# A Strassen GLU with a spectral branch on one core: an addition, a weight step, bank reads and SBUF additions change places in hand-ordered queues, and one tile gets a second buffer

## The chip, the cores and the metric

The kernel runs on one core of a Trainium2 chip. The metric is the device time of one execution in microseconds; the time before is 1399.58 us, the median of three runs (1398.88 to 1401.85). A core has five engines that each work through a queue in order: TensorE (PE; its weight loads are listed as PEld), VectorE (DVE), ScalarE (ACT), GpSimd (POOL) and SyncE (SP), which here only issues DMAs. Engines wait for one another through semaphores, so an instruction that waits holds up everything behind it in its queue.

## The reference

```python
xn = layernorm(A_x)                        # (1, 2048, 576), no affine part
a  = irfft2(rfft2(xn) * (w_r + 1j * w_i))  # over both axes
h  = sigmoid(xn @ w_gate) * (xn @ w_up)    # 576 -> 4608
out = A_x + a + h @ w_down                 # 4608 -> 576
```

All is float32. The kernel splits each fp32 operand into a high part (fp32r) and a low part, the difference to the high part, and multiplies high by high, low by high and high by low.

## The kernel before, in words

**Units.** The first stage makes h. F = 4608 is cut into 36 blocks f of 128, and the 2048 rows into two halves p, each as two column blocks of 512. A unit (f, p) makes both the gate and the up product for its block with seven products instead of eight (Strassen's scheme in Winograd's form): P1 to P7, each a group of seven matmuls of 128x512 (`prod`, L360). They gather in three PSUM banks: A (P1, then P2 on it), B (a copy of A after P1, then P6, P7 and P4 on it) and E (P5, then P3 on it). Banks A and E have two buffers, B one. `unit` (L393) writes the order out by hand: P5, P6, P2, P7, then P1 of the next unit (`ahead`), then P4 and P3. Between them ACT copies or squashes bank B and A into h and g (L401, L405, L408, L411, L418), and DVE adds bank E to h: L415 adds P5's part to h[:, 1], and P3, which adds onto bank E, must wait until it has been read; L421 adds E with P3 to h[:, 0]; L422 multiplies by g.

**Besides.** Seven times in a unit `beside()` (L838) is called, and whatever it emits takes its place in the engines' queues there. It advances `make_w(f + 1)` (L221), which splits the next block's weights: three ACT copies (L213), their low halves on DVE (L217, L219), then the sums in place (L229, L231, L232), four ACT copies more and the low halves of w1 and w2. Five steps of it come in unit (f, 0), the rest in (f, 1), two steps a beside in its first two. There are 31 units of p = 1 that lead to a new block. It also calls `tick()`, which takes one step of each side job: `export` (L425), which sends h, its sums and differences (L439, L442, L445, L448) to DRAM for two blocks at a time, and `make_t` (L452), which splits w_down's blocks (L465, L467, and L476 to L482) and sends them to DRAM. In the last two units it advances `early()` (L802) too: the first loads of the second stage, its first high and low parts (`cut_hi`, L793 and L796; `cut_lo`, L798 and L800). From the third unit on PE, DVE and ACT run in exactly the written order; for units (2, 0) and (3, 0) a scheduler orders the instructions. The last four units are (34, 0), (35, 0), (34, 1), (35, 1).

**The second stage** multiplies h by w_down in the same seven products, now one after another: for product j, half p and block pair k (18 of them) one step n (L1215). A step fetches a piece of h for step n + 10, makes the high part for step n + 4 (ACT) and the low part for step n + 3 (DVE), and does 12 matmuls of 128x288 in four PSUM banks m0 to m3, one buffer each (`down`, L1198). At k = 0 and 16 banks m0 and m1 are done for two steps at once, at k = 1 and 17 banks m2 and m3. So m0 and m1 end one step before m2 and m3, and a step later m0 and m1 are written again. A finished bank goes to `evac` (L1133): an addition or copy out of the bank first, and, one step later (`emptied`, L1210), additions from SBUF to SBUF (two per bank for P7 and P5, one for P2 and P6). They are all L1142.

Beside it, `aside()` advances the spectral branch: `phase1b` (L918), 16 tiles, with normalisation into xb (L285), the even and odd parts eo (L929, one buffer, read by PE's transposes pf), the high and low parts (L906, L909), products pd and pa; `phase2` (L982) with L1015, L1017 and L1019; `phase3` (L1035), whose L1098 to L1101 add the result to acc and so free the bank that py or pe takes next. `landed` (L897) sends a finished row block out.

Of the kernel before, what the change touches and what calls it, by code (L numbers as in the profile page):

```python
# [9 lines left out]
F32 = mybir.dt.float32  # L10
# [3 lines left out]
OP = mybir.AluOpType  # L14
PSUM = bass.MemoryType.PSUM

P = 128
# [107 lines left out]
def spectral_glu_kernel(ctx: ExitStack, tc: tile.TileContext, x, w_r, w_i, w_gate, w_up, w_down, out):  # L125
# [231 lines left out]
    STEPS = ((0, 0), (3, 0), (0, 3), (1, 1), (4, 1), (1, 4), (2, 2))  # L357
    H = {}

    def prod(b, w, xx, start, stop, skip=False):  # L360
        for j, (sx, sw) in enumerate(STEPS):
            nc.tensor.matmul(b, w[:, sw, :], xx[:, sx, :], start=start and j == 0, stop=stop and j == len(STEPS) - 1,  # L362
                             skip_group_check=skip)

# [16 lines left out]

    B = {}

    def made(u, b, k, start, stop=True):
        f, p = u
        ka, kb = FACTORS[k]
        prod(B[u, b], weight(f, kb), get_x(p, ka), start, stop, not start)

    def ahead(u):
        B[u, "A"] = bank("bA", f"pA{u[0]}_{u[1]}", 2)  # L390
# [2 lines left out]
    def unit(u, beside, after):  # L393

        f, p = u
        h = new_h(f, p)
        g = run.tile([P, 2, CW], F32, tag="g", name=f"g{f}_{p}")
        B[u, "B"] = bank("bB", f"pB{f}_{p}")
        B[u, "E"] = bank("bE", f"pE{f}_{p}", 2)
        bA, bB, bE = (B[u, k] for k in "ABE")  # L400
        nc.scalar.activation(bB, bA, AF.Copy)  # L401
        made(u, "E", "P5", True)
        beside()
        made(u, "B", "P6", False)
        nc.scalar.activation(h[:, 0], bB, AF.Copy)  # L405
        beside()
        made(u, "A", "P2", False)
        nc.scalar.activation(g[:, 0], bA, AF.Sigmoid)  # L408
        beside()
        made(u, "B", "P7", False)  # L410
        nc.scalar.activation(h[:, 1], bB, AF.Copy)  # L411
        beside()
        if after:
            ahead(after)
        nc.vector.tensor_tensor(h[:, 1], h[:, 1], bE, op=OP.add)  # L415
        beside()
        made(u, "B", "P4", False)
        nc.scalar.activation(g[:, 1], bB, AF.Sigmoid)  # L418
        beside()
        made(u, "E", "P3", False)  # L420
        nc.vector.tensor_tensor(h[:, 0], h[:, 0], bE, op=OP.add)  # L421
        nc.vector.tensor_tensor(h, h, g, op=OP.mult)  # L422
        beside()

    def export(k, p):  # L425

        a, b = H[2 * k, p], H[2 * k + 1, p]
        A11, A21, A12, A22 = a[:, 0], a[:, 1], b[:, 0], b[:, 1]

        def put(what, src):  # L430
            nc.sync.dma_start(ssp[ORDER.index(what)][p][k], src)

        put("P1", A11)
        put("P2", A12)
        put("P4", A22)
        s = run.tile([P, 2, CW], F32, tag="s", name=f"s{k}_{p}")
        S1, S2 = (s[:, i] for i in range(2))
        yield
        nc.vector.tensor_tensor(S1, A21, A22, op=OP.add)  # L439
        put("P5", S1)  # L440
        yield
        nc.vector.tensor_tensor(S2, S1, A11, op=OP.subtract)  # L442
        put("P6", S2)
        yield
        nc.vector.tensor_tensor(A21, A11, A21, op=OP.subtract)  # L445
        put("P7", A21)
        yield
        nc.vector.tensor_tensor(A12, A12, S2, op=OP.subtract)  # L448
        put("P3", A12)
        yield  # L450

    def make_t(k):  # L452
# [349 lines left out]
    def early():  # L802
        for n in range(20):
            if n < 2:
                for i in range(3):
                    fetch(3 * n + i)
            else:
                fetch_t(0, n - 2)
            if 12 <= n <= 12 + CA:
                cut_hi(n - 12)  # L810
            if 13 <= n < 13 + CA:
                cut_lo(n - 13)
            yield
        for n in range(FS, FA):
            fetch(n)
# [5 lines left out]
    for i, u in enumerate(UNITS):  # L821
        if i == 2:
            written.enter_context(tc.manual_schedule(engines={nc.tensor.engine, nc.vector.engine, nc.scalar.engine}))
        f, p = u
        after = UNITS[i + 1] if i + 1 < len(UNITS) else None
        last = f >= NF - 2
        if i == 0:
            sides += [export(0, 1), factors(1)]
            make = make_w(3)
        elif (f, p) == (3, 1) or (f > 3 and p == 0 and f + 1 < NF):  # L830
            make = make_w(f + 1)
        if (f, p) == (NF - 2, 1):
            first.close()
            ring = late.enter_context(tc.tile_pool(name="ring", bufs=1, side="right", reuse_waits="tile"))
            soon = early()
        count = 0

        def beside():  # L838
            nonlocal count
            count += 1  # L840
            turn = after and after[0] != f
            for _ in range(2 if turn and (last or f == 3 or count < 3) else 1 if turn or f < 4 or count > 2 else 0):
                next(make, None)
            for _ in range(2 if turn and (last or count < 4) else 1):
                next(soon, None)
            tick()
            if turn and count == 7:
                finish(make)
            if i == 1 and count == 4:
                finish(*sides)  # L850

        unit(u, beside, after)
        if f % 2 == 1:
            sides.append(export(f // 2, p))
        if u == (3, 0):
            load_raw(4)
            load_raw(5)
        elif p == 0 and f >= 4 and f + 2 < NF:
            load_raw(f + 2)
        if u == (2, 1):  # L860
            sides.append(g for k in range(NPR) for g in make_t(k))
# [56 lines left out]
    def phase1b(t):  # L918
# [5 lines left out]
        for _ in range(6):  # L924
            yield
        norm(xb[:, :D], acc[t], t)
        eo = wide(pool, "eo", t)
        for e, op in ((0, OP.add), (1, OP.subtract)):
            nc.vector.tensor_tensor(eo[:, e, :HD + 1], xb[:, :HD + 1], xb[:, HD:D + 1][:, ::-1], op=op)  # L929
        yield  # L930
# [202 lines left out]
    def evac(what, p, m, b):  # L1133

        v = b[:, :HD]
        t1, t2 = tid(p, 0, m), tid(p, 1, m)

        def part(q):
            return acc[(t1, t2)[q // 2]][:, q % 2 * HD:(q % 2 + 1) * HD]

        def add(o, a):
            nc.vector.tensor_tensor(o, o, a, op=OP.add)  # L1142

        if what == "P1":
            U[p, m] = u = accp.tile([P, HD], F32, name=f"u{p}{m}")
            nc.scalar.activation(u, v, AF.Copy)
        elif what == "P2":
            add(part(0), v)
            yield
            add(part(0), U[p, m])  # L1150
        elif what == "P6":
            add(U[p, m], v)
            yield
            add(part(1), U[p, m])
        elif what == "P7":
            add(U[p, m], v)
            yield
            add(part(2), U[p, m])
            add(part(3), U[p, m])
        elif what == "P4":  # L1160
            add(part(2), v)
        elif what == "P5":
            w = accp.tile([P, HD], F32, tag="v", name=f"v{p}{m}", bufs=4)
            nc.scalar.activation(w, v, AF.Copy)
            yield
            add(part(3), w)
            landed(t2)
            add(part(1), w)
        else:
            add(part(1), v)  # L1170
            landed(t1)
        yield

    active = []

    def aside():
# [21 lines left out]
    def down(n, m):  # L1198
        j, p, k = seq[n]
        if k == 0:  # L1200
            M[m] = ps.tile([P, CW], F32, tag=f"m{m}", name=f"m{j}_{p}{m}")
        s, t, o = SP_[n], TT[j, k], M[m][:, :HD]
        for i, (a, b) in enumerate(((0, 0), (0, 1), (1, 0))):
            nc.tensor.matmul(o, s[:, a, m * P:(m + 1) * P], t[:, b, :], start=k == 0 and i == 0, stop=k == NPR - 1 and i == 2)  # L1204
        if k == NPR - 1:
            done.append(evac(ORDER[j], p, m, M[m]))

    done, out_of = [], []

    def emptied():  # L1210
        out_of[:] = [g for g in out_of if next(g, out_of) is not out_of]
        out_of.extend(g for g in done if next(g, done) is not done)
        done.clear()

    for n, (j, p, k) in enumerate(seq):  # L1215
        fetch(n + FA)
        for load in loads.pop(n, []):
            load()
        if n:
            cut_hi(n + CA)  # L1220
            cut_lo(n + CA - 1)
        emptied()
        if k in (0, NPR - 2):
            for m in range(2):
                down(n, m)
                down(n + 1, m)
        elif k in (1, NPR - 1):
            for m in range(2, TPC):
                down(n - 1, m)
                down(n, m)  # L1230
        else:
            for m in range(TPC):
                down(n, m)
        active.extend(b() for b in begin.pop(n, []))
        aside()
    while active or done or out_of:
        emptied()
        aside()
    assert not begin and not loads, (begin, loads)
    written.close()  # L1240
    two.close()
# [21 lines left out]
```

## Time and profile before

| | |
|---|---|
| median of the runs | 1399.58 us |
| the profiled execution | 1399.83 us |
| its span, first to last instruction | 1398.0 us |
| matmuls | 7827 |
| HBM over the span | 211 GB/s |

The span is cut as follows: up to about 105 us the start, hand-ordered but for its end; to about 856 us the units; after that the second stage with the spectral branch. In the lines of the timeline the first number is the start in us from the span's start, the second the length in us, then engine, line, operation and tiles, `xN` the number of instructions merged, and in brackets how long the engine stood before it and for whom. In the lines of waits: total in us, number, longest. In the lines by stage: stretch, length, then busy us and number of instructions of PE, PEld, DVE, ACT and POOL, granted clock of PE, share of the DMA engines, GB/s. The group lines of the page give busy us and mean ns, then the idle time ahead of them and who ended it. DVE's instructions overlap a little: the distance from start to start is shorter than the length shown.

### The profile page before, as it was taken

What the parts mean: (1) busy time and instruction counts of PE and PEld (TensorE: products, weight loads), DVE (VectorE), ACT (ScalarE), POOL (GpSimd) and SP (SyncE); (2) the same over time, 40 slices, a digit from 0 to 9 for tenths busy, and PEclk for the clock granted to TensorE, in tenths of its full rate; (3) what the DMA queues carried; (4) which work ended last, traced back from release to release, by engine and by line L of the source; (5) the groups of instructions that cost most, each with busy time, mean ns of one, the idle gap of its engine ahead of it and who ended that gap; (6) DMA issues with size and microseconds to landing.
All of it is one profiled execution on the core that took longest, in us unless ns stands there. A gap on an engine that the chain in (4) does not pass through costs nothing.

```text
span 1398.0 us, 22544 instructions
## 1 busy us (share of the span) xinstructions
PE 1377.5 (99%) x7827; PEld 1219.6 (87%) x7827; DVE 963.2 (69%) x1768; ACT 706.6 (51%) x1432; POOL 19.5 (1%) x39
## 2 busy tenths in 40 slices
PE   9999999999999999999999999999999999999998
PEld 7788887788887888888788878999999999999998
DVE  8785668676776677666777665666767777756664
ACT  5553444444444444444444433565557767645553
POOL 4000000000000000000000000000000000000000
PEclk9999999999999999999999999999999999999999
DMA  7033555555554465545564449996899989988761
GB/s 242 24 108 114 182 202 195 195 170 191 199 207 157 167 216 193 197 162 193 198 209 164 155 147 348 329 330 210 257 296 281 303 274 310 309 277 285 240 194 58
DMA packets 221538, 296.76 MB, mean 212 GB/s; under 512 B 18545, under 2 KB 124401, under 8 KB 221169
## 3 DMA queue, kind: packets, MB, share of 16 engines
q1 hardware_dynamic: 221280, 295.26, 63.9%
q8 instruction: 62, 1.02, 0.3%
q14 instruction: 52, 0.42, 0.1%
q10 hardware_dynamic: 144, 0.07, 0.0%
HBM read 177.82 MB, written 117.44 MB: 211 GB/s over the span
## 4 chain that ended last, share of the span: by engine, by line
PE 87%; DVE 8%; DMA 2%; issue 2%; ACT 1%; SPq 0%; DVEq 0%; ACTq 0%
PE m L1204 26%; PE pB L362 21%; PE pE L362 16%; PE pA L362 14%; PE pd L963 2%; PE pe L1092 2%; PE py L1055 1%; PE pa L976 1%; PE pc L1029 1%; PE pb L1007 1%; DMA acc<-in_A_x 1%; DVE xs L329 1%; DVE w L217 1%; DMA sc<-u 1%; DVE st L245 1%
## 5 line engine op out<-in xcount | busy, mean ns | idle before, releaser
L1204 PE MATMUL m<-tt,sp 128*128 128x288 f32 x3024 | 415.9, 294 | 4.7 <-DVE u L1142 2.8
L1204 PEld LDWEIGHTS m<-tt,sp 128*128 128x128 f32 x3024 | 403.2, 188 | 6.0 <-DVE u L1142 3.5
L800 DVE TENSOR_TENSOR sp<-sf,sp 128x512 fp32r<-128x512 f32 x252 | 169.2, 688 | 23.9 <-ACT sp L796 22.3
L796 ACT ACTIVATE sp<-sf 128x512 fp32r<-128x512 f32 x252 | 155.3, 629 | 48.8 <-PE m L1204 24.9
L213 ACT ACTIVATE w<-raw 128x384 fp32r<-128x384 f32 x238 | 113.1, 515 | 99.8 <-DVE raw L229 98.1
L362 PE MATMUL pA<-X1A,w 128*128 128x512 f32 x518 | 130.3, 390 | 0.0
L362 PE MATMUL pE<-X1S,w 128*128 128x512 f32 x490 | 123.9, 392 | 4.2 <-DVE h L415 4.1
L362 PE MATMUL pA<-X0A,w 128*128 128x512 f32 x490 | 124.0, 390 | 0.0
L362 PE MATMUL pE<-X0S,w 128*128 128x512 f32 x490 | 123.9, 391 | 0.1
L421 DVE TENSOR_TENSOR h<-h,pE 128x512 f32<-128x512 f32 x68 | 46.8, 688 | 108.5 <-PE pE L362 108.4
L362 PE MATMUL pB<-X1S,w 128*128 128x512 f32 x476 | 120.6, 392 | 0.1
L362 PE MATMUL pB<-X0S,w 128*128 128x512 f32 x476 | 119.4, 389 | 0.0
L362 PEld LDWEIGHTS pE<-X1S,w 128*128 128x128 f32 x490 | 91.1, 188 | 26.7 <-DVE h L415 7.9
L362 PEld LDWEIGHTS pA<-X1A,w 128*128 128x128 f32 x518 | 97.0, 188 | 20.0
L362 PEld LDWEIGHTS pE<-X0S,w 128*128 128x128 f32 x490 | 91.7, 188 | 19.6 <-DVE h L415 0.5
L362 PEld LDWEIGHTS pA<-X0A,w 128*128 128x128 f32 x490 | 91.8, 188 | 19.4 <-ACT pB L401 0.5
L362 PEld LDWEIGHTS pB<-X1S,w 128*128 128x128 f32 x476 | 88.4, 188 | 22.7 <-ACT h L405 3.9
L362 PEld LDWEIGHTS pB<-X0S,w 128*128 128x128 f32 x476 | 89.2, 188 | 18.7 <-ACT h L405 0.2
L418 ACT ACTIVATE g<-pB 128x512 f32<-128x512 f32 x68 | 40.7, 598 | 128.1 <-PE pB L362 128.1
L405 ACT ACTIVATE h<-pB 128x512 f32<-128x512 f32 x68 | 40.1, 590 | 122.3 <-PE pB L362 118.8
L415 DVE TENSOR_TENSOR h<-h,pE 128x512 f32<-128x512 f32 x68 | 46.6, 685 | 75.4 <-ACT h L411 75.3
L422 DVE TENSOR_TENSOR h<-h,g 128x1024 f32<-128x1024 f32 x68 | 83.3, 1225 | 7.0
(202 smaller groups left out, 1878.5 us busy)
## 6 DMA issues: line engine op xcount, KB each, us to landing
sf<-ss SPq DMA_DIRECT2D x252, 256.0 KB
ss<-h SPq DMA_DIRECT2D x180, 256.0 KB
ts<-tP SPq DMA_DIRECT2D x126, 288.0 KB
tt<-ts SPq DMA_DIRECT2D x126, 288.0 KB
ss<-s SPq DMA_DIRECT2D x72, 256.0 KB
wd<-in_B_w_down SPq DMA_DIRECT2D x36, 288.0 KB
raw<-in_B_w_gate SPq DMA_DIRECT2D x72, 128.0 KB
raw<-in_B_w_up SPq DMA_DIRECT2D x72, 128.0 KB
```

Source lines behind the costliest of these rows:

```text
L213: nc.scalar.activation(o[:, i, :3, :], src[:, i], AF.Copy)
L362: nc.tensor.matmul(b, w[:, sw, :], xx[:, sx, :], start=start and j == 0, stop=stop and j == len(STEPS) - 1, skip_group_check=skip)
L405: nc.scalar.activation(h[:, 0], bB, AF.Copy)
L415: nc.vector.tensor_tensor(h[:, 1], h[:, 1], bE, op=OP.add)
L418: nc.scalar.activation(g[:, 1], bB, AF.Sigmoid)
L421: nc.vector.tensor_tensor(h[:, 0], h[:, 0], bE, op=OP.add)
L422: nc.vector.tensor_tensor(h, h, g, op=OP.mult)
L796: nc.scalar.activation(s[:, 0], SF[n], AF.Copy)
L800: nc.vector.tensor_tensor(SP_[n][:, 1], SF[n], f32(SP_[n][:, 0]), op=OP.subtract)
L963: nc.tensor.matmul(pd[:, e, :NQ], l, r, start=n == 0, stop=n == len(steps) - 1)
L1092: nc.tensor.matmul(pe[:, e, :NQ], l, r, start=n == 0, stop=n == len(steps) - 1)
L1204: nc.tensor.matmul(o, s[:, a, m * P:(m + 1) * P], t[:, b, :], start=k == 0 and i == 0, stop=k == NPR - 1 and i == 2)
```

## The change

- In a unit, L415 goes from behind the fourth beside and the next unit's P1 to directly behind the copy L411. The seventh beside goes ahead of L421 and L422.
- In the last unit, which has no next P1, the last three matmuls of P2 and the gate's sigmoid go behind P7 and the fourth beside.
- The last exports write A12 - S2 to a tile of its own and not over A12.
- `early` makes one low part more (step 4's), and the loop's first low part begins a step later.
- Unit (34, 0) takes no side step in its first two besides.
- eo has two buffers.
- A step of the second stage reads finished banks first, then makes the high and low parts. The additions from SBUF go to a list, `slow`, and one of them is popped at the end of each step.

```diff
@@ made, prod: an argument `which` picks some of the seven matmuls
@@ unit
         made(u, "B", "P6", False)
         nc.scalar.activation(h[:, 0], bB, AF.Copy)
         beside()
-        made(u, "A", "P2", False)
-        nc.scalar.activation(g[:, 0], bA, AF.Sigmoid)
+        if after:
+            made(u, "A", "P2", False)
+            nc.scalar.activation(g[:, 0], bA, AF.Sigmoid)
+        else:
+            made(u, "A", "P2", False, which=range(4))
         beside()
         made(u, "B", "P7", False)
         nc.scalar.activation(h[:, 1], bB, AF.Copy)
+        nc.vector.tensor_tensor(h[:, 1], h[:, 1], bE, op=OP.add)
         beside()
         if after:
             ahead(after)
-        nc.vector.tensor_tensor(h[:, 1], h[:, 1], bE, op=OP.add)
+        else:
+            made(u, "A", "P2", False, which=range(4, len(STEPS)))
+            nc.scalar.activation(g[:, 0], bA, AF.Sigmoid)
         beside()
         made(u, "B", "P4", False)
         nc.scalar.activation(g[:, 1], bB, AF.Sigmoid)
         beside()
         made(u, "E", "P3", False)
+        beside()
         nc.vector.tensor_tensor(h[:, 0], h[:, 0], bE, op=OP.add)
         nc.vector.tensor_tensor(h, h, g, op=OP.mult)
-        beside()
@@ export
-        nc.vector.tensor_tensor(A12, A12, S2, op=OP.subtract)
-        put("P3", A12)
+        o = run.tile([P, 2, CW], F32, tag="g", name=f"o{k}_{p}")[:, 0] if apart else A12
+        nc.vector.tensor_tensor(o, A12, S2, op=OP.subtract)
+        put("P3", o)
@@ early
-            if 13 <= n < 13 + CA:
+            if 13 <= n <= 13 + CA:
                 cut_lo(n - 13)
@@ beside
-            tick()
+            if u != (NF - 2, 0) or count > 2:
+                tick()
...
-            sides.append(export(f // 2, p))
+            sides.append(export(f // 2, p, not after))
@@ phase1b
-        eo = wide(pool, "eo", t)
+        eo = wide(pool, "eo", t, 2)
@@ evac: for P2, P6, P7, P5 alike
             add(U[p, m], v)
-            yield
-            add(part(2), U[p, m])
-            add(part(3), U[p, m])
+            slow.append(lambda: add(part(2), U[p, m]))
+            slow.append(lambda: add(part(3), U[p, m]))
@@ the loop over steps
+    def read_out():
+        for what in done:
+            evac(*what)
         done.clear()
+
+    def catch_up():
+        if slow:
+            slow.pop(0)()
...
+        read_out()
         if n:
             cut_hi(n + CA)
+        if n > 1:
             cut_lo(n + CA - 1)
-        emptied()
...
         aside()
+        catch_up()
```

More of the change, by code (lines that the diff above doesn't have):

```diff
@@ L358, in spectral_glu_kernel, with prod @@
     H = {}
-    def prod(b, w, xx, start, stop, skip=False):
-        for j, (sx, sw) in enumerate(STEPS):
+    def prod(b, w, xx, start, stop, skip=False, which=range(len(STEPS))):
+        for j in which:
+            sx, sw = STEPS[j]
             nc.tensor.matmul(b, w[:, sw, :], xx[:, sx, :], start=start and j == 0, stop=stop and j == len(STEPS) - 1,
@@ L382, in spectral_glu_kernel, with made @@
     B = {}
-    def made(u, b, k, start, stop=True):
+    def made(u, b, k, start, stop=True, which=range(len(STEPS))):
         f, p = u
         ka, kb = FACTORS[k]
-        prod(B[u, b], weight(f, kb), get_x(p, ka), start, stop, not start)
+        prod(B[u, b], weight(f, kb), get_x(p, ka), start, stop, not start, which)
     def ahead(u):
@@ L420, in unit, with export @@
         made(u, "E", "P3", False)
+        beside()
         nc.vector.tensor_tensor(h[:, 0], h[:, 0], bE, op=OP.add)
         nc.vector.tensor_tensor(h, h, g, op=OP.mult)
-        beside()
-    def export(k, p):
+    def export(k, p, apart=False):
         a, b = H[2 * k, p], H[2 * k + 1, p]
@@ L1148, in evac @@
             add(part(0), v)
-            yield
-            add(part(0), U[p, m])
+            slow.append(lambda: add(part(0), U[p, m]))
         elif what == "P6":
             add(U[p, m], v)
-            yield
-            add(part(1), U[p, m])
+            slow.append(lambda: add(part(1), U[p, m]))
         elif what == "P7":
             add(U[p, m], v)
-            yield
-            add(part(2), U[p, m])
-            add(part(3), U[p, m])
+            slow.append(lambda: add(part(2), U[p, m]))
+            slow.append(lambda: add(part(3), U[p, m]))
         elif what == "P4":
@@ L1164, in evac, with lower @@
             nc.scalar.activation(w, v, AF.Copy)
[L1165 to L1168, printed above, removed]
+            def lower():
+                add(part(3), w)
+                landed(t2)
+            slow.append(lower)
+            slow.append(lambda: add(part(1), w))
         else:
@@ L1171, in evac @@
             landed(t1)
-        yield
+    slow = []
     active = []
@@ L1205, in down @@
         if k == NPR - 1:
[L1206 to L1212, printed above, removed]
+            done.append((ORDER[j], p, m, M[m]))
+    done = []
+    def read_out():
+        for what in done:
+            evac(*what)
         done.clear()
+    def catch_up():
+        if slow:
+            slow.pop(0)()
     for n, (j, p, k) in enumerate(seq):
@@ L1235, in spectral_glu_kernel @@
         aside()
-    while active or done or out_of:
-        emptied()
+        catch_up()
+    while active or done or slow:
+        read_out()
         aside()
+        catch_up()
     assert not begin and not loads, (begin, loads)
```

## The prediction

> **What bounds the kernel now.** I read the page first, then busy time by stage, then the waits of TensorE's weight load (PEld), and last the timeline around each kind of wait.
>
> ```profile
> span 1398.0 us, 22544 instructions
> PE 1377.5 (99%) x7827; PEld 1219.6 (87%) x7827; DVE 963.2 (69%) x1768; ACT 706.6 (51%) x1432; POOL 19.5 (1%) x39
> ```
>
> ```profile
> 105.00:850.00 745.00, 740.16 (x3236) 604.88 (x3235) 511.04 (x823) 328.17 (x685) 0.10 (x1) 1.00 0.54 184
> 850.00:1398.00 548.00, 537.66 (x4071) 533.76 (x4069) 367.64 (x746) 321.47 (x635) 0.00 (x0) 1.00 0.84 268
> ```
>
> TensorE is busy for 99% of the span at a granted clock of 1.00. The change removes no matmul, so all it can give is TensorE's own waits: about 5 us idle in the units (105 to 850) and 10 us after them, the tail among it, plus what a stopped pipeline loses while it fills. In the second stage the weight load is as full as the matmuls (533.76 of 548), so a wait there costs what PEld waits. These are those waits, with total, times and longest; the first four are from 105 to 870, the others after 870:
>
> ```profile
> PEld pE L362 <- DVE h L415: 8.4, 10, 1.6
> PEld pB L362 <- ACT h L405: 4.1, 10, 0.4
> PEld pB L362 <- ACT h L411: 2.6, 4, 1.1
> PEld m L1204 <- DVE sp L800: 1.6, 1, 1.6
> ```
>
> ```profile
> PEld m L1204 <- DVE u L1142: 3.5, 3, 1.7
> PEld pa L976 <- issue: 1.8, 4, 0.4
> PEld m L1204 <- DVE acc L1142: 0.8, 1, 0.8
> PEld py L1055 <- issue: 0.4, 2, 0.2
> ```
>
> Every line but the last is one that an edit touches directly. No other is over 0.5 us between 105 us and the tail.
>
> **h's addition behind its copy.** P3 adds into bank pE, so it must wait until L415 has read it. One such place, in units of p = 1 that lead to a new weight block:
>
> ```profile
> 264.40 1.75 PE L362 MATMUL pA<-X0A,w 128*128 128x512 f32 x7
> 264.60 0.60 ACT L411 ACTIVATE h<-pB 128x512 f32<-128x512 f32 x1 [0.35 <-PE pB L362]
> 265.99 1.75 PE L362 MATMUL pB<-X1A,w 128*128 128x512 f32 x7
> 266.08 0.68 DVE L217 TENSOR_TENSOR w<-raw,w 128x512 fp32r<-128x512 f32 x1
> 267.81 0.68 DVE L415 TENSOR_TENSOR h<-h,pE 128x512 f32<-128x512 f32 x1
> 268.55 0.98 PE L362 MATMUL pE<-X1S,w 128*128 128x512 f32 x3 [0.81 <-DVE h L415]
> ```
>
> Groups of seven matmuls follow each other every 1.59 us (264.40 to 265.99), so P3 was due at 267.58 and came at 268.55: 0.97 lost. The copy L411 was finished at 265.20; L415 stood behind the besides' work that begins with L217, not behind the copy. In L217's place it starts at 266.08 and ends at 266.76, before 267.58. The wait goes.
>
> What does one event cost in all? The smallest are seen with the other wait of this stage, P7 on the copy out of bank pB (L405):
>
> ```profile
> 167.74 0.69 DVE L421 TENSOR_TENSOR h<-h,pE 128x512 f32<-128x512 f32 x1 [1.76 <-PE pE L362]
> 169.68 0.95 DVE L229 TENSOR_TENSOR raw<-raw 128x768 f32<-128x768 f32 x1
> 170.66 0.94 ACT L213 ACTIVATE w<-raw 128x384 fp32r<-128x384 f32 x2 [3.30 <-DVE raw L229]
> 170.72 1.75 PE L362 MATMUL pA<-X1A,w 128*128 128x512 f32 x7
> 172.47 1.89 PE L362 MATMUL pB<-X1S,w 128*128 128x512 f32 x7
> 174.20 1.76 PE L362 MATMUL pA<-X0A,w 128*128 128x512 f32 x7
> ```
>
> ```profile
> PE pE L362 <- DVE h L415: 4.1, 6, 1.2
> L421 DVE TENSOR_TENSOR h<-h,pE 128x512 f32<-128x512 f32 x68 | 46.8, 688 | 108.5 <-PE pE L362 108.4
> ```
>
> Spacings of 1.75 and 1.73 against 1.59 make 0.30 us, though PE shows no idle time: refilling. So L415's ten events cost 4.1 + 10 x 0.30 = 7.1. I take 7.0 as gained; bounds 4.1 (only shown idle) and 7.1.
>
> The price of the move: VectorE now stands at L415 until the copy is there, and the besides' work waits behind it: the low halves of w2, one or two additions of an export or a weight block, the DMAs on SP that wait for these. The low halves are needed by P6 of the next unit, four groups or 6.3 us later; the exports go to DRAM for the second stage. VectorE has 745 - 511 = 234 us free in this stage, which is the cover. POOL does nothing here (0.10 us).
>
> **Weights' sums sooner.** The seventh beside moves ahead of L421 and L422. It issues L229 (0.95) and one step of the side work, and in the last units loads for the second stage; on SP nothing changes places, since L421 and L422 issue no DMA. VectorE idles 108.5 / 68 = 1.6 us before each L421, so L229 fits; with a 0.45 side step L421 may be late by tenths, and it reads a bank that has a second buffer. In the rows above ACT stood 3.30 us for L229; with L229 done before 167.74 the two L213 run some 3 us earlier and L405, which came behind them, follows P6 at once. The ten events at 0.30 go: 3.0, of which I take 2.7.
>
> **Units (34,0) and (35,1).**
>
> ```profile
> 816.91 0.69 DVE L439 TENSOR_TENSOR s<-h,h 128x512 f32<-128x512 f32 x1
> 817.52 0.95 DVE L229 TENSOR_TENSOR raw<-raw 128x768 f32<-128x768 f32 x1
> 819.57 1.89 PE L362 MATMUL pB<-X0A,w 128*128 128x512 f32 x7 [0.55 <-ACT h L411]
> ```
>
> ```profile
> 852.64 1.88 PE L362 MATMUL pB<-X1A,w 128*128 128x512 f32 x7 [0.69 <-ACT h L411]
> ```
>
> Without side steps in its first two besides, (34,0) has no L439 ahead of L229: what follows comes 0.61 sooner, so of 0.55 + 0.30 about 0.2 stays; its export's stores leave SP two besides (3.2 us) later, and nothing among the units reads them. In the last unit, three matmuls of P2 (3 x 1.59 / 7 = 0.68) go behind P7 and cover that much of the copy: 0.7 of 0.99. Together 1.4.
>
> **From units to the second stage.**
>
> ```profile
> 862.67 0.69 DVE L448 TENSOR_TENSOR h<-h,s 128x512 f32<-128x512 f32 x1 [2.44 <-DMA ss<-h]
> 863.28 3.70 DVE L800 TENSOR_TENSOR sp<-sf,sp 128x512 fp32r<-128x512 f32 x6
> ```
>
> L448 overwrites A12 in place and waits 2.44 for the DMA that sends A12 out, with the low halves behind it. Written to a tile of its own (the last unit's g, free since L422) it doesn't wait, and the low half that PE stood for is made in the last unit already. Next late would be the half after it, wanted 12 matmuls (1.6 us) later and freed 2.4 sooner. The whole 1.6 goes; I take 1.5.
>
> **Even and odd parts in two buffers.**
>
> ```profile
> 904.07 0.83 DVE L929 TENSOR_TENSOR eo<-xb 128x289 f32<-128x289 f32 x2 [3.34 <-PE pf L941]
> 905.42 1.86 DVE L909 TENSOR_TENSOR al<-pd,ah 64x290 fp32r<-64x290 f32 x4
> ```
>
> L929 held VectorE 3.34 us until the transposes had read the only buffer; the four L909 behind it end at 907.28, too late for pa. Free of this they start as soon as ACT has written ah, a step's length sooner. All four waits of pa go: 1.8. The second buffer costs SBUF and no instruction.
>
> **Banks read first, SBUF additions from a queue.**
>
> ```profile
> 1125.31 0.88 DVE L1015 TENSOR_TENSOR z<-wr,pb 128x512 f32<-128x512 f32 x3
> 1126.11 0.90 DVE L1017 TENSOR_TENSOR t<-wi,sw 128x512 f32<-128x512 f32 x3
> 1126.91 0.69 DVE L800 TENSOR_TENSOR sp<-sf,sp 128x512 fp32r<-128x512 f32 x1
> 1127.51 1.56 DVE L1142 TENSOR_TENSOR acc<-acc,u 128x288 f32<-128x288 f32 x4
> 1128.99 0.82 DVE L1142 TENSOR_TENSOR u<-u,m 128x288 f32<-128x288 f32 x2
> ```
>
> Two banks are read in one step (ending where L1015 starts, 1125.31), the other two in the next (1128.99), and PE waits for the latter. The new order puts the low half L800 behind the reads in both steps. That takes 0.60 out of the stretch before the second pair, but the L800 of the step before, which ran while VectorE stood for PE, comes into it: a net of nothing. Of the four SBUF additions (1.48, 0.37 each) one stays, popped at the end of the step. So the second pair starts at 1125.31 + 0.60 + 0.80 + 0.80 + 0.37 = 1127.88, 1.11 sooner. The other three events have two additions there: 0.37 sooner each. Sum 2.2, and 0.1 for one with small gaps: 2.3 of 4.3; the rest stays. P5's additions are spread too, which frees L1098 and with it py: 0.4.
>
> [...]
>
> **Sum.** 7.0 + 2.7 + 1.4 + 1.5 + 1.8 + 2.3 + 0.4 = 17.1 from the profiled execution's 1399.83 (span 1398.0), so 1382.7; that execution is within 0.3 of the median of the runs shown, 1399.58. Units (2,0) and (3,0) are ordered by the scheduler and may come out differently; I bound that by one wait of the kind above (0.30 to 0.97), either way, and allow 0.3 for it: 1383.0.
>
> **Rivals.** (a) The waits of the unit stage are handed on: what now stands behind L415 or runs ahead of L421 makes another copy or weight half late, and 9.7 us (7.0 + 2.7) come back as tenths elsewhere: about 1392.5. For it: side work stood in the queue wherever a wait arose. Against: 234 us free, 6.3 us of slack.
>
> (b) The DMA engines bound the second stage: their share is 0.84 over it, and then 1.5 + 1.8 + 2.3 + 0.4 = 6.0 gained there are paid back waiting for DRAM: 1389.0. Against it: no row of PEld's waits after 870 names a DMA. [...]
>
> (c) Slower: VectorE, parked at L415, doesn't finish the side work in time for the next weights' low halves, and TensorE waits once in each of the 31 units that lead to a new block. At the 0.97 of the row above that is 30 us, less the 7.4 that go elsewhere (1.4 + 6.0): about 1422. It decides when the work between L415 and the next unit's P6 passes 6.3 us; in the rows at hand it is about 3.
>
> (d) The queue's order isn't the cause of the P3 waits, and L415 is late anyway because its copy is: 7.0 less, 1390. L411's end at 265.20 against L415's start at 267.81 speaks against it.
>
> **How the numbers follow.** Forecast 0.76, own range 1380 to 1387 (the term bounds: P3's lower one costs 2.9, banks with nothing gained 2.3, the scheduler 1.0 either way; banks wholly cured 2.0 less). (a) 0.09, (b) 0.06, (d) 0.04, (c) 0.03, a near-cancelling mix of them 0.02. The range takes in (b) and (d) and half a microsecond for the runs' own spread: 1379.5 to 1390.5. About 0.2%, 2.8 us, is what a measurement of this kernel can tell from no change: faster 0.95 (all but the last two), same 0.02, slower 0.03.
>
> **What would show it.** In the new profile: no wait of pE for L415 nor of pB for L405; L229 ahead of L421 in time; L448's last one without a DMA wait and PE idle under 0.3 around 860; L929 without waits for pf, pa without waits; three m waits of about 0.5 to 0.6 and a smaller fourth left, released by L1142. The prediction is wrong if DVE waits at L415 grow and PEld waits for w appear, or if PE's idle time from 105 to 850 stays near 5 us.

## The result and the profile after

The changed kernel took 1383.68 us against 1399.42 for the kernel before, a ratio of 0.9879 [0.9866, 0.9892]. (One of its four runs took 1690.4 us at a granted clock of 0.753 and is left out of the ratio; the other three took 1382.55 to 1384.08, median 1383.29.) Run once more, beside other runs of the kernel before, it took 1382.04 (1381.27 to 1383.93), ratio 0.9867 [0.9853, 0.9882]. The forecast was 1383.0, range 1379.5 to 1390.5.

Its page opens as follows:

```profile
span 1382.3 us, 22539 instructions
PE 1371.2 (99%) x7827; PEld 1222.6 (88%) x7827; DVE 962.2 (70%) x1768; ACT 712.1 (52%) x1432; POOL 20.1 (1%) x39
```

The matmuls are as many as before and PE's busy time is nearer to the span: 11.1 us of idle time are left of 20.5. By stage, with the columns of before:

```profile
105.00:840.00 735.00, 735.00 (x3241) 607.47 (x3240) 511.17 (x825) 333.95 (x687) 0.10 (x1) 1.00 0.54 187
840.00:1382.30 542.30, 536.41 (x4071) 533.50 (x4069) 368.12 (x746) 321.17 (x635) 0.00 (x0) 1.00 0.85 270
```

PE has no idle time at all in the units. These are all waits from 105 us on, PE's first, then PEld's (total, times, longest):

```profile
PE pd L972 <- DVE fl L918: 1.0, 1, 1.0
PE m L1213 <- DVE u L1151: 1.0, 3, 0.3
PE m L1213 <- DVE acc L1151: 0.2, 1, 0.2
```

```profile
PEld m L1213 <- DVE u L1151: 1.7, 3, 0.6
PEld pB L363 <- ACT h L415: 1.4, 4, 0.4
PEld pd L972 <- DVE fl L918: 1.2, 1, 1.2
PEld m L1213 <- DVE acc L1151: 0.5, 1, 0.5
PEld pB L363 <- ACT h L406: 0.4, 2, 0.2
PEld pB L363 <- DVE w L219: 0.2, 1, 0.2
PEld pa L985 <- issue: 0.2, 1, 0.2
```

Line numbers have moved: the copy L411 is L415 here, h's addition L416, the other addition L429, the matmuls of the second stage L1213, the additions L1151. No wait for h's addition is left, 0.4 of 4.1 for the copy (L406), 1.4 of 2.6 for the other copy (L415 here, L411 before), half of the waits of m, a tenth of those of pa, none of py. A wait of pd has grown, from 0.4 in the weight load to 1.2.

To part the stages, all kernels below are compared at one point, the first product of the second stage. In the timelines of PE it stands here, before and after:

```profile
855.95 2.27 PE L1204 MATMUL m<-tt,sp 128*128 128x288 f32 x16
```

```profile
845.26 12.93 PE L1213 MATMUL m<-tt,sp 128*128 128x288 f32 x97
```

So 10.7 us were gained before this point and 1398.0 - 855.95 = 542.1 against 1382.3 - 845.26 = 537.0, or 5.1, behind it. One loss in the first part has nothing to do with the change: in the start, ahead of all that was edited, seven matmuls took 3.31 us in the changed kernel's profile and 1.85 in the profile of before:

```profile
57.72 3.31 PE L363 MATMUL pA<-X1A,w 128*128 128x512 f32 x7
```

```profile
57.87 1.85 PE L362 MATMUL pA<-X1A,w 128*128 128x512 f32 x7
```

The same kernel was run again for this:

> The changed kernel once more, as it is, to have its time on the chip of the two kernels beside it and a second profile. If the wait of pd for fl of 1.36 belongs to the program, it is in this profile too; if it hangs on when the load of cf lands, it can be gone or have another size. The same for the dip of the granted clock near 58 us that cost 1.47 in the first profile: in the spans of this kernel's runs it should separate two groups 1.4 to 1.6 apart. Time 1382.5 to 1384.1, ratio near 0.988.

Its profile has no such dip of the clock (granted clock over 40 to 60 us 1.00, against 0.94 in the first profile), a wait of pd of 0.7 (PE) or 0.9 (PEld), and its first product starts at 843.74: 12.2 gained before that point, 5.4 behind it. This profile stands for the changed kernel in the comparisons below.

| kernel | median us (range) | ratio to before | first product at | from there to the end |
|---|---|---|---|---|
| before | 1399.42 (1398.88-1401.85) | 1 | 855.95 | 542.1 |
| changed, again | 1382.04 (1381.27-1383.93) | 0.9867 [0.9853, 0.9882] | 843.74 | 536.7 |
| addition alone | 1395.47 (1394.27-1397.47) | 0.9967 [0.9955, 0.9980] | 850.96 | 541.4 |
| beside alone | 1391.10 (1390.03-1391.73) | 0.9933 [0.9919, 0.9947] | 845.90 | 543.5 |
| the rest alone | 1392.48 (1391.80-1392.80) | 0.9944 [0.9931, 0.9956] | 854.10 | 536.2 |
| addition undone | 1382.40 (1382.15-1383.92) | 0.9875 [0.9859, 0.9892] | 844.32 | 536.0 |
| edge undone | 1383.88 (1383.70-1385.94) | 0.9887 [0.9873, 0.9900] | 843.69 | 538.4 |
| eo with one buffer | 1383.79 (1383.20-1384.50) | 0.9883 [0.9869, 0.9896] | 843.75 | 537.7 |
| no queue | 1385.99 (1385.26-1386.67) | 0.9894 [0.9879, 0.9908] | 845.61, dip | 538.8 |
| cuts first | 1382.99 (1381.48-1383.20) | 0.9875 [0.9861, 0.9888] | 845.58, dip | 535.5 |
| between free | 1379.18 (1378.77-1380.58) | 0.9852 [0.9838, 0.9865] | 845.58, dip | 533.2 |
| between free, eo one | 1382.34 (1380.76-1382.79) | 0.9864 [0.9847, 0.9880] | 845.42, dip | 535.5 |
| between free, cf in pieces | 1381.37 (1381.12-1382.73) | 0.9868 [0.9853, 0.9884] | 843.65 | 535.7 |

The ratios stand against runs of before on the same chip; their intervals reach about 2 us to either side. The medians of different rows come in part from different chips. "Dip" says that the clock of the profile dipped in the start as above (0.94 to 0.96 over 40 to 60 us, 1.00 in the others), which puts the first product 1.5 to 1.9 us later. The last two columns come from one profile each and tell apart what the medians cannot.

### The profile page after: what moved, and what is told of

Its sections match the earlier page's. It is cut to its first block, busy times and chain, and to the rows that moved or that the text cites. A ratio compares the mean times of both kernels' runs of the same rounds, so it can differ in the third digit from the quotient of the medians.

```text
span 1382.3 us, 22539 instructions
## 1 busy us (share of the span) xinstructions
PE 1371.2 (99%) x7827; PEld 1222.6 (88%) x7827; DVE 962.2 (70%) x1768; ACT 712.1 (52%) x1432; POOL 20.1 (1%) x39
## 4 chain that ended last, share of the span: by engine, by line
PE 90%; DVE 4%; DMA 3%; SPq 1%; issue 1%; ACT 1%; DVEq 0%; ACTq 0%
PE m L1213 26%; PE pB L363 23%; PE pE L363 16%; PE pA L363 16%; PE pd L972 2%; PE pe L1101 2%; PE py L1064 1%; PE pc L1038 1%; PE pa L985 1%; PE pb L1016 1%; DMA tt<-ts 1%; DMA ss<-s 1%; DMA acc<-in_A_x 1%; DVE xs L329 1%; PE pz L1079 1%
## 5 line engine op out<-in xcount | busy, mean ns | idle before, releaser
L1213 PE MATMUL m<-tt,sp 128*128 128x288 f32 x3024 | 415.6, 294 | 1.2 <-DVE u L1151 1.0
L1213 PEld LDWEIGHTS m<-tt,sp 128*128 128x128 f32 x3024 | 403.1, 188 | 2.2 <-DVE u L1151 1.7
L416 DVE TENSOR_TENSOR h<-h,pE 128x512 f32<-128x512 f32 x68 | 46.7, 687 | 148.0 <-ACT h L415 138.8
L406 ACT ACTIVATE h<-pB 128x512 f32<-128x512 f32 x68 | 40.7, 598 | 169.2 <-PE pB L363 165.8
L213 ACT ACTIVATE w<-raw 128x384 fp32r<-128x384 f32 x238 | 113.9, 517 | 22.8 <-DVE raw L229 19.8
L217 DVE TENSOR_TENSOR w<-raw,w 128x512 fp32r<-128x512 f32 (+1 forms) x103 | 80.0, 777 | 5.2 <-ACT w L213 4.4
```

The source lines that it names most:

```text
L213: nc.scalar.activation(o[:, i, :3, :], src[:, i], AF.Copy)
L217: eng.tensor_tensor(o[:, :, 3:, :], src[:, :, :KT, :], f32(o[:, :, :KT, :]), op=OP.subtract)
```

## The experiments

**The two edits of the unit.** My theory put 7.0 us to h's addition and 2.7 to the seventh beside. A rival that I formed on seeing the trace after: both edits cure the same backlog on VectorE, and either takes the other's gain.

Addition alone, on the kernel before:

```diff
         nc.scalar.activation(h[:, 1], bB, AF.Copy)
+        nc.vector.tensor_tensor(h[:, 1], h[:, 1], bE, op=OP.add)
         beside()
         if after:
             ahead(after)
-        nc.vector.tensor_tensor(h[:, 1], h[:, 1], bE, op=OP.add)
```

> The kernel before with one part of the change: L415 directly behind its copy. Theory (each wait of the units belongs to one edit, as the prediction's sum has it): the ten waits of P3 for L415 go, the ten of P7 for L405 stay at 0.30 us each; 7.0 us less than before, ratio 0.995. Rival (overlap: side work ahead of L415 in the queue makes the P3 waits, and either edit takes enough of it away): the same here, 0.995; the two differ in the run with the seventh beside alone. Rival (handed on): P7's waits grow or waits for weights appear, and the gain is under 3 us.

All its waits went, but the first product came only 5.0 us sooner (855.95 - 850.96), neither the theory's 7.0 nor under 3. The waits for the copy L411 grew from 2.6 to 3.6, those for the copy L405 from 4.1 in ten to this:

```profile
PEld pB L362 <- ACT h L405: 6.5, 13, 0.8
```

The 1.0 more for L411 is one wait at the end of the first two units, which the scheduler orders and ordered otherwise here:

```profile
110.74 1.64 PE L362 MATMUL pB<-X0A,w 128*128 128x512 f32 x6 [0.69 <-ACT h L411]
```

Before, the same group started at 109.62 without a wait. Matched matmul by matmul, this kernel is 0.3 us ahead of the one before at 108 us and 0.7 behind at 114. So about 1.0 of the 2.0 us that are missing belongs to the scheduler's order; the prediction had bounded that by one such wait, either way. The rest came back in tenths at L405. One place shows how:

```profile
365.33 0.69 DVE L412 TENSOR_TENSOR h<-h,pE 128x512 f32<-128x512 f32 x1 [1.78 <-ACT h L411]
...
369.82 0.68 DVE L421 TENSOR_TENSOR h<-h,pE 128x512 f32<-128x512 f32 x1
370.60 1.23 DVE L422 TENSOR_TENSOR h<-h,g 128x1024 f32<-128x1024 f32 x1
371.74 0.95 DVE L229 TENSOR_TENSOR raw<-raw 128x768 f32<-128x768 f32 x1
372.73 0.94 ACT L213 ACTIVATE w<-raw 128x384 fp32r<-128x384 f32 x2 [3.64 <-DVE raw L229]
373.91 0.58 ACT L405 ACTIVATE h<-pB 128x512 f32<-128x512 f32 x1
374.54 1.65 PE L362 MATMUL pB<-X1S,w 128*128 128x512 f32 x6 [0.35 <-ACT h L405]
```

VectorE stands 1.78 us at the addition until its copy is there. L421 then starts without a wait for PE: VectorE is behind. L229 follows two instructions later, ACT stands 3.64 us for it with the copy L405 behind, and PE waits 0.35. That is rival (a) of the prediction in small: about 1 of 7 us.

Beside alone, on the kernel before:

```diff
         made(u, "E", "P3", False)
+        beside()
         nc.vector.tensor_tensor(h[:, 0], h[:, 0], bE, op=OP.add)
         nc.vector.tensor_tensor(h, h, g, op=OP.mult)
-        beside()
```

> The kernel before with another part alone: the seventh beside ahead of L421 and L422. Theory (each wait belongs to one edit): P7's ten waits for L405 go, P3's ten for L415 stay; 2.7 us less, ratio 0.998. Rival (overlap): L229 and a side step leave the stretch ahead of L415, which so starts 0.95 to 1.25 us sooner; P3 idled for L415 by 0.01 to 1.16 us, so eight or nine of its ten waits go as well, and the two longest shrink to about 0.2; 8.6 us less, ratio 0.994.

The first product came 10.0 us sooner (855.95 - 845.90): this edit alone gives as much as both terms together (9.7). The ratio, 0.9933, is the rival's 0.994 and not the theory's 0.998. Before, VectorE had stood idle in front of L421, with L229 behind it:

```profile
258.25 0.69 DVE L421 TENSOR_TENSOR h<-h,pE 128x512 f32<-128x512 f32 x1 [1.13 <-PE pE L362]
...
260.19 0.95 DVE L229 TENSOR_TENSOR raw<-raw 128x768 f32<-128x768 f32 x1
```

The same unit with the beside moved (L421 is L422 here):

```profile
255.02 0.95 DVE L229 TENSOR_TENSOR raw<-raw 128x768 f32<-128x768 f32 x1
...
256.26 0.68 DVE L422 TENSOR_TENSOR h<-h,pE 128x512 f32<-128x512 f32 x1
...
264.50 0.68 DVE L415 TENSOR_TENSOR h<-h,pE 128x512 f32<-128x512 f32 x1
```

and PE there:

```profile
265.56 1.75 PE L362 MATMUL pE<-X1S,w 128*128 128x512 f32 x7
```

L229 and the side step of its beside fill the idle time, and from L421 to h's addition VectorE needs 264.50 - 256.26 = 8.2 us where it needed 267.81 - 258.25 = 9.6. The addition ends at 265.18, and P3 starts at 265.56 without a wait, though the addition stands in its old place behind all the side work.

The rest alone (the changed kernel with the two diffs above taken back):

> The changed kernel with both edits of the unit undone: h's addition (the L415 of before) stands behind the next unit's P1 again, and the seventh beside behind the two additions. All else of the change stays. By the terms of the prediction, what is left is 1.4 + 1.5 + 1.8 + 2.3 + 0.4 = 7.4, less what the wait of pd for fl costs now (about 0.9 more than before in the profile of the changed kernel): 1399.4 - 7.4 + up to 0.9 = about 1392.0 to 1392.9, a ratio near 0.995, with ten waits of P3 for the addition and ten of P7 for the copy back in the units. The overlap theory (the seventh beside and the addition cure the same waits) says the same of the sum: together they gave 15.7 - 7.4 = 8.3 to 9.7. A rival: the edits of the second stage gain less than their terms, and those of the units more; then this kernel is at 1395 or above.

The first product starts at 854.10, 1.85 us sooner than before, and the second part takes 536.2. The pair is therefore worth 854.10 - 843.74 = 10.4 us. Alone the two gave 4.99 + 10.05 = 15.04, so 4.7 of it is the same gain twice, and more if the 1.0 us of the scheduler's units is not counted against the addition.

Addition undone (the changed kernel with the first of the two diffs taken back):

> The changed kernel with h's addition alone put back behind the next unit's P1; the seventh beside stays ahead of the two last additions. If each edit cured the waits that the prediction put down to it, the ten waits of P3 are back, 7.0 slower than the changed kernel: 1389.0 to 1390.7. If the seventh beside cures nearly all of both (it took 10.0 us from the units by itself, the pair 10.4), a few of them are left, 1.3 in the weight load as there: 0.3 to 1.5 slower, 1382.4 to 1385.2, and the first product of the second stage starts within 1.5 us of the changed kernel's 843.7 (845.3 with the dip of the clock).

The waits for it in the weight load, and the first product:

```profile
PEld pE L363 <- DVE h L422: 0.8, 2, 0.5
```

```profile
844.32 13.85 PE L1213 MATMUL m<-tt,sp 128*128 128x288 f32 x104
```

Two small waits, 844.32 - 843.74 = 0.6 us, and a time within the other's range: with the beside moved, the addition's place is worth 0.6, not 7.0. The worth hangs on the order: with the addition moved first, 10.4 - 5.0 = 5.4 are left for the beside. The changed kernel with the beside alone undone was not run.

**From units to the second stage.** Edge undone (the changed kernel, minus these two; of the exports only the last unit's is changed):

```diff
-            if 13 <= n <= 13 + CA:
+            if 13 <= n < 13 + CA:
...
-        if n > 1:
+        if n:
             cut_lo(n + CA - 1)
...
-            sides.append(export(f // 2, p, not after))
+            sides.append(export(f // 2, p))
```

> The changed kernel with the last export overwriting A12 in place again, and step 4's low part made in the second stage again and not in the last unit; the split of P2 and the later side steps of unit (34, 0) stay. By the prediction's term a wait of m for the low part of 1.3 to 1.6 is back near 850 to 860 us: 1.5 slower than the changed kernel, about 1385.2. A rival: the low halves' queue has moved on since the units end on time, so the wait is under 0.5 and the time that of the changed kernel, 1383.7.

The wait came back larger than it had been. VectorE and PE:

```profile
851.47 0.69 DVE L456 TENSOR_TENSOR h<-h,s 128x512 f32<-128x512 f32 x1 [3.50 <-DMA ss<-h]
```

```profile
852.82 3.43 PE L1213 MATMUL m<-tt,sp 128*128 128x288 f32 x24 [2.38 <-DVE sp L808]
```

L456 waits 3.50 for the DMA where L448 waited 2.44 before, and PE stands 2.38. Counted from the first product, L456 starts at 851.47 - 843.69 = 7.8 us and L448 started at 862.67 - 855.95 = 6.7: PE has come forward by more than the transfer. The median, 1383.88, is near the rival's 1383.7 and does not decide: against the changed kernel's own runs it is 0.2 or 1.8 us slower (1383.68, 1382.04). The profile does: the second part took 538.4 against 536.7, and as the wait of pd (below), 0.9 there, is absent here, the two undone edits are worth 2.6 us. No run parts one from the other.

**eo with one buffer**, tried twice, on the changed kernel and on the best one:

```diff
-        eo = wide(pool, "eo", t, 2)
+        eo = wide(pool, "eo", t)
```

> The changed kernel with one buffer for the even and odd parts. By the prediction's term the four waits of pa are back, four of about 0.47 of the weight load: 1.8 slower than the changed kernel, about 1385.5, ratio near 0.989, and the addition that writes eo stands over 3 us for the transposes. A rival: with the bank reads ahead and the SBUF additions in a queue the four products of al end in time anyway, so that the buffer is worth under 0.5: 1383.7 to 1384.2 with no wait of pa.

> The best kernel (e5_between_free, 1379.2) with one buffer for the even and odd parts. The same question as e6_eo_one, where the times were equal though four waits of pa were back, because the wait of pd for fl was in one profile and not in the other. By the prediction's term this kernel is 1.8 to 2.0 slower than e5_between_free: 1381.0 to 1381.2. A rival: the time is e5_between_free's again, 1379.2, and the buffer is worth nothing.

In the first of them:

```profile
889.84 0.83 DVE L938 TENSOR_TENSOR eo<-xb 128x289 f32<-128x289 f32 x2 [3.36 <-PE pf L950]
```

```profile
PEld pa L985 <- issue: 1.9, 5, 0.4
```

VectorE's stand (3.34 before) and the waits of pa (1.8 in four) are back to within a tenth. The second part takes 537.7, less the changed kernel's 536.7 without its 0.9 for pd: 1.9. In the second pair of kernels it is 535.5 - 533.2 = 2.3, of which 0.4 is a wait of pd. The term of 1.8 holds by the profiles. The medians alone would not have shown it: 1383.79 stands 0.1 above the changed kernel's first runs and 1.75 above its second ones, and the second pair's lie 3.2 apart for 1.8 to 2.0 expected.

**Banks and queue.** Cuts first (the changed kernel, finished banks read behind both cuts again):

```diff
-        read_out()
         if n:
             cut_hi(n + CA)
         if n > 1:
             cut_lo(n + CA - 1)
+        read_out()
```

> The changed kernel with the high and low parts of each step ahead of the bank reads again, the queue of SBUF additions kept. Theory (the low part that leaves the stretch before the second pair of banks is paid back by the one that enters it): m's four waits stay as they are after the change, 0.2 to 0.35 us idle each; the time of the changed kernel, ratio to before 0.988. Rival (reading the banks first is what shortened the waits): each of the four waits grows by 0.60, 2.4 us more than the changed kernel, ratio 0.990.

No queue (the changed kernel; the step before's SBUF additions run at once, ahead of the reads):

```diff
     def read_out():
+        while slow:
+            slow.pop(0)()
         for what in done:
             evac(*what)
         done.clear()
...
     def catch_up():
-        if slow:
-            slow.pop(0)()
+        pass
```

> The changed kernel without its queue: all SBUF additions of the step before run in one go ahead of the next two finished banks, as before the change; the banks are still read ahead of the high and low parts. The prediction took the whole of its 2.3 us for the banks from the queue and nothing from the reads' new place. By that the four waits of m are back at their old size, 4.3 in place of the 2.3 left: 2.0 slower than the changed kernel run beside it. A rival: the reads' new place carries it, since the low part runs behind them; then the waits and the time are those of the changed kernel, within 0.5.

Cuts first leaves the four waits of m exactly as they are (PEld 1.7 in three and 0.5 in one). No queue has the waits of before, and those of py:

```profile
PEld m L1213 <- DVE u L1151: 3.5, 3, 1.7
PEld m L1213 <- DVE acc L1151: 0.8, 1, 0.8
PEld py L1064 <- issue: 0.4, 2, 0.2
```

So the reads' new place gives nothing and the queue gives 4.3 - 2.2 = 2.1 of m and 0.4 of py. The second part is 538.8 - 536.7 = 2.1 longer, and 3.0 without the changed kernel's 0.9 for pd; some 0.5 of that is in no wait named here. The medians of the two, from one chip, lie 3.9 apart (1385.99 and 1382.04), more than either expectation, 2.0 or under 0.5; a dip of 1.5 in some of the runs can be part of that, and the rest is not explained. The rows at the largest wait stand in the order that the prediction worked out. No queue, then the changed kernel:

```profile
1113.52 1.55 DVE L1151 TENSOR_TENSOR acc<-acc,u 128x288 f32<-128x288 f32 x4
1114.99 0.81 DVE L1151 TENSOR_TENSOR u<-u,m 128x288 f32<-128x288 f32 x2
```

```profile
1111.25 0.69 DVE L808 TENSOR_TENSOR sp<-sf,sp 128x512 fp32r<-128x512 f32 x1
...
1113.45 0.46 DVE L1151 TENSOR_TENSOR acc<-acc,u 128x288 f32<-128x288 f32 x1
1113.82 0.82 DVE L1151 TENSOR_TENSOR u<-u,m 128x288 f32<-128x288 f32 x2
```

Between the two reads stand still a low part (0.60) and one popped addition (0.37). Between free takes both away: at k = 17 the cuts run ahead of the reads, elsewhere behind, and at k = 17 nothing is popped.

```diff
-        read_out()
+        if k != NPR - 1:
+            read_out()
...
             cut_lo(n + CA - 1)
+        if k == NPR - 1:
+            read_out()
...
-        catch_up()
+        if k != NPR - 1:
+            catch_up()
```

> The changed kernel with both low parts kept out of the stretch between the two pairs of bank reads (ahead of the reads at k = 17, behind them in every other step) and no SBUF addition popped at k = 17. Theory (what stands between the two pairs is what PE waits for): the second pair starts 0.97 us sooner, more than the 0.60 that each of the four waits costs; all four go, 2.3 us less than the changed kernel, ratio to before 0.986. Rival (too few banks: one buffer each): the waits of m stay, ratio 0.988.

The reads of the second pair and PE at the same place:

```profile
1109.98 0.81 DVE L1151 TENSOR_TENSOR u<-u,m 128x288 f32<-128x288 f32 x2
1110.71 0.68 DVE L808 TENSOR_TENSOR sp<-sf,sp 128x512 fp32r<-128x512 f32 x1
```

```profile
1106.23 5.96 PE L1213 MATMUL m<-tt,sp 128*128 128x288 f32 x44
```

PE runs 44 products through, and no wait of PE is left anywhere after 105 us (of PEld's, 2.0 us are left, all in the units). The second part took 533.2 against 536.7: 2.2 for m, 0.9 for the wait of pd that is absent here, 0.2 for pa, 0.2 unexplained. This is the best kernel of the study, 1379.18 us, ratio 0.9852 [0.9838, 0.9865]. The rival of too few banks is out: with one buffer a bank, as before, the four stalls, 4.3 us in the kernel before, went by the order of VectorE's work alone.

**The wait of pd.** In the changed kernel's chain of waits and its timelines:

```profile
857.34 10.29 DMA acc<-in_A_x
```

```profile
867.65 0.58 DVE L285 TENSOR_SCALAR xb<-acc,mv,rstd 128x576 f32<-128x576 f32 x1 [5.88 <-DMA acc<-in_A_x]
```

```profile
870.96 0.40 PE L972 MATMUL pd<-cf,fl 128*128 128x290 f32 x1 [0.99 <-DVE fl L918]
```

A row block's load, issued 1.06 us behind that of cf (1.6 MB), takes 10.29 us, and everything of that row block starts late. (PE's wait is 0.99 in this row and PEld's 1.2; the 1.36 of two expectations is too much.) I tried to cure it on the best kernel:

```diff
-        for _ in range(4):
+        src = con["cf"].rearrange("p (e k n) -> p e k n", e=2, k=5)
+        for k in range(5):
+            load_r(cf[:, :, k], src[:, :, k])
             yield
-        load_r(cf, con["cf"].rearrange("p (e k n) -> p e k n", e=2, k=5))
-        yield
```

> The best kernel so far (the changed one with its finished banks read between the high and the low part, e5_between_free, 1379.2) with the 1.6 MB load of cf cut into five loads, one per step from the first step on, and not one load after four steps. In the changed kernel's profile an issue on SP (of the accumulators, L931) stood 3.6 us until this load had landed, VectorE stood 5.9 behind it, and PE waited 1.36 for it at 871 us. If the size of the load is the cause, no such wait comes in any execution: 1379.2 or up to 1 us less, since it was absent in the profile of e5_between_free too. A rival: the wait comes from the amount of data ahead and not from its pieces; then the time is the same or, as the pieces start sooner and run against the first step's loads, up to 1.5 us more.

It is worse than either expectation: 1381.37, with the wait of pd still there (0.9) and a second one, of pf for rp, of 1.3. Smaller pieces, started sooner, stand ahead of an earlier row block's load as well: it was issued 856.14 - 843.65 = 12.5 us behind the first product, in the changed kernel 854.31 - 845.26 = 9.1, and VectorE stood 4.49 us for it where the best kernel's did not.

The size of the wait goes with the time of the load behind cf. Five profiles show both, all with the edge edits and cf in one piece. From the load's issue to VectorE's start on that row block 8.1, 8.6 and 9.1 us pass where PEld does not wait for fl (cuts first, eo with one buffer, between free), 10.1 and 10.3 where it waits 0.9 and 1.2 (the changed kernel, second and first profile). Why the same load takes up to 2 us longer in one profile than in another stays open.

## Why the prediction was right, and which step failed

**What bounds the kernel.** Right: PE's waits were all there was to gain, most of them are gone, and the time is the forecast's within 1 us. The DMA share went from 0.84 to 0.85, and only the wait of pd, behind a late load, took 0.5 to 0.8 of the 6.0 back, so rival (b) came in small at most. (c) did not come: VectorE does stand longer at h's addition, but PE doesn't follow. The group on the page and that of ACT's copies, before and after:

```profile
L415 DVE TENSOR_TENSOR h<-h,pE 128x512 f32<-128x512 f32 x68 | 46.6, 685 | 75.4 <-ACT h L411 75.3
L213 ACT ACTIVATE w<-raw 128x384 fp32r<-128x384 f32 x238 | 113.1, 515 | 99.8 <-DVE raw L229 98.1
```

```profile
L416 DVE TENSOR_TENSOR h<-h,pE 128x512 f32<-128x512 f32 x68 | 46.7, 687 | 148.0 <-ACT h L415 138.8
L213 ACT ACTIVATE w<-raw 128x384 fp32r<-128x384 f32 x238 | 113.9, 517 | 22.8 <-DVE raw L229 19.8
```

VectorE idles 148.0 / 68 = 2.2 us before each addition, 75.4 / 68 = 1.1 before. The prediction had named growing waits there, together with waits for w, as a sign against itself; only the first came (one wait for w, 0.2). It is the free time that used to lie before L421, moved: that went from 108.5 to 38.9 us. ACT's idle time for L229 went from 98.1 to 19.8 us, in line with the prediction's "some 3 us earlier" (78.3 over 31 units is 2.5).

**Addition 7.0 and beside 2.7: the split failed, the sum held.** The pair gave 10.4 for a forecast of 9.7. The sum held because the pair took away nearly all of both lines of waits, 8.4 and 4.1 in PEld, whichever edit cures which; that says nothing for the split. For one edit alone the forecast would have been out by 2.0 (5.0 for 7.0) or 7.3 (10.0 for 2.7). The step that failed is "In L217's place it starts at 266.08 and ends at 266.76, before 267.58. The wait goes.", taken as the edit's own worth: it priced each edit by the waits that bear its line's name. (The prediction's 0.30 us for each event is the spacing in the rows, 1.75 and 1.73 us against 1.59; that PE refills in that time is the author's reading and not shown.) Why the side work ahead of L415 was late was not asked. It was late because L229 and a side step stood behind the idle time before L421, which the prediction had in hand (1.6 us a unit) and used as cover only. With the beside moved first it is worth 10.0 and the addition 0.6; with the addition first, 5.0 and, by difference, 5.4. Rival (d), the addition late because its copy is late, was wrong; rival (a) was right for a kernel with the addition alone, for about 1 of 7 us.

**(34, 0) and (35, 1) 1.4, and 0.3 allowed for the scheduler.** The rest alone gained 1.85 before the first product, 0.45 more than the term and 0.75 more than term and allowance. No part of it was run by itself, but its matmuls can be matched with those of before: the group at 817.27 comes 0.32 sooner, the one at 824.82, behind unit (34, 0)'s wait, 1.26, and the one at 852.64, the last unit's, 1.85. So the two units gave 0.9 and 0.6 for the 0.65 and 0.7 that the prediction's rows make. The scheduler's units, for which 0.3 was set aside, took nothing in the changed kernel: it is 0.15 ahead at 94 us and 0.35 at 126. With the pair's 0.7 this makes the 12.2 measured before that point out of 10.8 forecast.

**From units to the second stage 1.5.** Mechanism right. Against the kernel before, no more than its wait of 1.6 can have come of it. In the changed kernel the edits are worth 2.6: with the units' waits gone the same DMA is later against PE, and without them 1.0 of the units' gain would have been lost here.

**Even and odd parts 1.8.** Right: 1.9 measured twice.

**Banks and queue 2.3, py 0.4.** Right in each step: nothing from the reads' place, 2.1 and 0.4 from the queue, and at the largest wait the rows 1111.25 to 1113.82 give the 2.57 us that were added up. Three waits of about 0.6 and one of 0.5 are left, as forecast.

**What was missing.** The wait of pd for fl, 0.4 before, is 1.2 and 0.9 us in the two profiles of the changed kernel, and 1.3 with the beside alone; the prediction left it out as small. With it the second part gained 5.1 to 5.4 us for 6.0 forecast (1.5 + 1.8 + 2.3 + 0.4). The waits add up to nearly that in the second profile: 1.6 of m for the low part, 1.6 of pa, 2.1 of m and 0.4 of py gone, 0.5 of pd more, 5.2 for 5.4 measured.

**Luck.** The units gave 1.4 more than forecast and the second part 0.6 to 0.9 less. That the time came out within 1 us of the forecast is in part that these two offset each other. The upper end of the own range, 1387, is also less than its bounds add up to (1383.0 + 2.9 + 2.3 + 1.0 = 1389.2); nothing hung on it.

## What to carry to other kernels

A wait's name tells which instruction came last, not which edit cures it (the beside moved alone gave 10.0 us, the waits put down to it 2.7): before pricing two edits of one queue separately, ask what made that queue late, and test each alone and each undone. Two edits that cure the same waits have a sum, but no worth of their own: it hangs on which comes first (h's addition gave 5.0 us by itself, 0.6 with the beside moved). Free time in front of an instruction that waits in an in-order queue is a cheap place for the work behind it; here one moved call alone took 10.0 us from the units, of the 12.2 that the whole change took there. When the busiest engine's waits go, price the next wait at the new start times, since the same transfer can then be later against it (with the edge undone VectorE stood 3.50 us for the DMA for which it stood 2.44 before).

## What the runs showed of the hardware

The granted clock dipped in some executions of the same kernel and not in others. Here are 40 to 60 us in the first profile of the changed kernel, at 0.94, and in the second, at 1.00 (the granted clock is the third number from the end):

```profile
40.00:60.00 20.00, 18.00 (x90) 14.26 (x91) 14.47 (x41) 10.28 (x20) 0.52 (x1) 0.94 0.07 27
```

```profile
40.00:60.00 20.00, 17.98 (x97) 14.39 (x98) 14.46 (x41) 10.65 (x22) 0.52 (x1) 1.00 0.08 27
```

In windows of 1 us from 57 to 62 the first profile's clock reads 0.85, 0.50 three times and 0.95. Ahead of the dip PE has two idle gaps of 0.75 and 0.78 us with only short transposes between and behind them: one group of products ends at 52.59 + 1.75 = 54.34 and the next starts at 57.72. The profile of the kernel before has like gaps (0.78 and 0.77), the same 3.4 us between the groups (52.72 + 1.75 = 54.47 to 57.87) and no dip, 1.00 in each window of 1 us from 54 to 62, so the gaps alone don't decide it; what does is not shown. The spans of the best kernel's runs part by the clock, 1378.8 at 0.999 and 1377.0 to 1377.4 at 1.000, but those of the changed kernel's second runs do not, against what was expected: 1379.5 and 1382.1 at 0.999, 1380.0 and 1380.5 at 1.000.
